# Another listed order for every step of a linear-attention and top-2 expert kernel

## The chip, the cores and the metric

The kernel runs on one core of a Trainium2 chip. The metric is the device time of one execution, in microseconds; less is better. Each version is run several times and compared by its median.

## The reference

The reference has two halves. First comes linear attention with a learned feature map, for 8 batches of 8 heads, 576 positions and 64 channels. Then a layer of four attention experts, of which the gate keeps two for each position:

```python
def phi(x):                       # 64 channels -> 256 features
    proj = einsum('bhsd,df->bhsf', x, w_phi)
    proj = proj - max(abs(proj), axis=-1)
    return concatenate([exp(proj), exp(-proj)], axis=-1)
kv  = einsum('bhsf,bhsd->bhfd', phi(k), v);  z = phi(k).sum(axis=2)
x   = einsum('bhsf,bhfd->bhsd', phi(q), kv) / (einsum('bhsf,bhf->bhs', phi(q), z) + 1e-6)
x   = x.transpose(0, 2, 1, 3).reshape(8, 576, 512)

w   = softmax over the 2 largest of x @ w_gate        # 4 experts
for e in range(4):
    a   = softmax(causal(0.125 * (x @ wq[e]) @ (x @ wk[e]).T))
    out += w[..., e] * (a @ (x @ wv[e]) @ wo[e])
```

All arrays are float32, and the output is 8 x 576 x 512.

## The kernel before, in words

The heads go in 32 pairs, four pairs to a batch. For a pair, TensorE projects the keys (`stream_k`, matmuls of `half_mm` at L501), VectorE centers them (`center`), ScalarE takes the exponentials (`phi_k`), and TensorE multiplies them with the values (`stream_kv`, L642). The last 64 keys of each head go two pairs at a time through `stream_tails` (also L501) and `tail_products` (L607). The sum over keys is needed too. For the first four pairs (batch 0) TensorE makes it from all keys. From pair 4 on `key_sum` makes most of it elsewhere: gpsimd starts a transfer that adds one half of the keys' features into `zs` (a transfer `zs<-ek`), VectorE adds two parts of `zs` (L582), gpsimd adds the tails (a transfer `zs<-ekt`), and TensorE only sums the result over partitions (L654). For the queries, TensorE projects (`stream_q`, L501), ScalarE or VectorE copies the result out (`evac_u`), gpsimd reduces over partitions, and two exponentials follow (`phi_q`). TensorE then makes denominators and numerators (`stream_n`, L740 and L751), and `divide` writes a pair's part of x.

When four pairs are done, `stream_b` projects the batch's x to q and k (`proj_t`) for two experts at a time, makes their scores (`scores`, L871), and projects v and the gate (`proj_v`). These projections and the last one to the output run through the helper `mm` (L294). Two experts' scores make a group, so there are 16 groups, 0 to 15. A group's causal scores lie in four sets of two PSUM banks, one bank an expert (`BANKS`): the first set has 512 columns, the second 256, the third 320, and the last 512, of which the last 64 count in 64 rows only. `evac_s` copies each bank to `s`; `mask` (gpsimd) fills the upper triangle; `maxima` takes a running maximum over key blocks (VectorE, L992), reduces it over partitions (gpsimd, L996) and subtracts it (VectorE, L1000); `expo` takes the exponentials in place (ScalarE, L305); `add_up` (VectorE, L1012) and `sums` (TensorE, L1038) make the divisor; `attend` multiplies with v (TensorE, L1067), `evac_y` scales and splits the result, and `project_out`, `evac_o` and `store` bring it out.

All of PSUM is one pool of eight banks of 512 float32 (`ps_c`). A step that needs a bank gets the one that was released longest ago, by the plan's own reckoning; TensorE waits if the copy that empties it is not done. Until the first x is complete, `keep_warm` multiplies a tile of ones in bursts of three matmuls.

The order of the work is written down. Each piece of work is a generator, and each `yield` in it is a step on one engine. `ORDER` is a string with one character a step, the place of the generator in the list of live ones. `SIDES` has one character for each copy that may go to ScalarE (0) or VectorE (1). `Plan.loop` (L225) replays both; a change to one character would change the meaning of all behind it, since a generator that ends leaves the list. `in_order` (L245) then pins each engine's instructions in the order in which they were made:

```python
for c in ORDER:
    s = self.streams[ord(c) - 48]
    st = s[1]
    if isinstance(st.eng, tuple):
        st.eng = st.eng[int(next(sides))]
```

Transfers are issued by SP, the first two loads of q by ScalarE, and the adding transfers by gpsimd. Each engine works through its own list and waits by semaphores for the data that it needs from the others.

Of the kernel before, what the change touches and what calls it, by code (L numbers as in the profile page):

```python
# [68 lines left out]


ORDER = (
    r'111111110432049269C8GD4FF79FCB53DDD2D987CEG0FIE8=D4H9B1FDBBHFF9DIHFEF=C=8I7JIFH99EFI5CL0CL8B2DBBB=D=E=EED>4B36'
    r'7=BIK=ICE8=HIIHDGEG>DGGEF5:>:2>9=I:KJCHBE=7:F=DBD:9:JF25DGFH=F=:FED>8H2>>E446:HHHJHHADB<7HHG8:5<AG:3H9JFMBBFBJ'
    r'A9GFCE0FA;<<88@:CE;7JACCIG<LI:CC;7@GI993::6KDJKHH:IDHD?BA:DGG??:;?9;GEEGF0DD;AGEEADD40CC@B?B01<96877;;;DA?=C4;'
    r'GHH8D=G=6==852;8:@30C>8IAD?CCCC?BC998CB;;6D>BF?CAF@GGCBE8A9F408F58A77FJ8IDJ?F;88KFFJ;3;BPLLH?JKB=HH18;GC;;:I;H'
    r'BIHHHCCCH6;JJ;2828BHH>6G@BGF8;5;>D=EECC=::8DHGHCGCC::<G>GFDE@H999JCJC?C03888808IC8HKJI:@68P8BHBFCIK<LBED7H5FIJ'
    r'JE83IF7IJF?K>FF:999=8JJLG?LE>C=88>A8=7EIJ?28AGA7BEGHII=FI8GG139>9>?6H9EHD8J8F75B4I87L<G20G?CK@DDFGGD<8<FE86H=G'
    r'8?D998:86?DHHIJG::IJJ<HI:7K7I:L:?M<C<IDC?F>????H:B>JKMK<;;MJ;8BJILL<FD:G:=8HIFLLI:JH::J58E86H0I8813KKIFA:L@IHN'
    r'H:>EIEII<EGEL<IDFGDEE=DE=DH;;<D:H:<ICKKIH@KGH>HFF<E6<<GDD@DDDDFDEEEE<K:CK:DIMLLG:20488N98ND?DL8EHLKI::5LMCC==L'
    r'FDPB<TI3AFQRBGL8LLFG9?990BBGD>FHHHDDLB8@E>;@@8@HB@AHJBB@AEC8@?CI=ABC>AEB982;;@7<7@DH88FE8=E>>>GFGD<DC83997=D8?'  # L80
    r'?88JI5GGH2B76?LFA8KHIH8F8H8LF9BE98GGJKKK8K;GIII1DEH=F5778083CH488=EHM2<D6JHKE6FA<I?IDH8CH::::::J98EHHKHD6:HL?G'
    r'HIJCHHDGFEGG99CH?BH88EFE7E?8GGE:8G88:GE?:J@7IGLI?G5BF:CKNPMMF@J=22=83180AFAA9;B;:::JCJECGB=D:E:JFL>K0FEECEKDCD'
    r'6GLJ<FIGEI?FE<<<<:DC<?NHHHFDGDCHCDED88:I=HGD::IFJBC>E8<<HB:JEDJEIF6D5LE9989G8K88347O7BCFKJH8EKCGCD;@KIG<M??MJH'
    r'C8GG688OCAKBGDG0J8=KA9998AID@32DH@DA57GING>GIJJJ>AE>JGLKFGG@>>>E848>E80I899F7DK>IBDFJDCC7E@=F=8;;=D==G9DCNED88'
    r'88L<FB57J6OL?I6MMJ3GJH<<:CGH:::0818282:OC:NEBDC=NMNDCCCJFI99:IFCHCFHH:FF7FA7;I8LH8CJICFE8IK::LE8:LML>5LFGCEE=:'
    r'6:EDB==NIKIKLNKEL<GC::GGJCBCGI:FC;;98=8=FG1D=DD=83C88F8DEBBFEFBH8I56E<8J=BKJJE=B6E?EEBB<<<@<B=@@::E99CCDFCC@88'
    r'48LLDK@;9CBMF=2>:G:A80388KH=KMFK=CJI88D83:<JCG?6@E99KCLL?8KCE977KLILL57IJLI8MN88D8HI72IM8LH88N<MKH9L@BGFCCL@GG'
    r'J9>920K<LKIDE?B=GG=F7H:<:<>:H=<L?KLAD::LIJF=KEI7L65D=DDDGE99K=DJFII77<DLFM6JJOKEC==CD=:K:<<G<<BG<ABL388488NL1M'
    r'KHFLM0<8CLEN8>8A8J56CNQNQ>GB80;;8F=AI8DE883IGHCJ::KO28KD;:LFD>LDDFGK:::DD=:QI:J6J@DCGFN=DFGIF:>>JDFCKHCEDHD9;;'
    r'688:DDDC=EGGEDCFF@:8IGC<:D5KD::FL<CONAKALALECCCOONKFAAO@<C>B=MAE@DNG@<H<DAAAA?LAA<??99DHAFGI@81B3DM20HF848C889'  # L90
    r'@IJCE?C<GB<HIHF>8A8AB87>DF>8C7;H5IFED6MA@MF<F<<G?99KC8<3F8I89?820JKJ8>4D<KFH88?>GDEGGE77999>L8>LF<CCFCD57DJLAG'
    r'2@3081>88LDEGEE8D<>ECC8FC9;;IDGB7B6ECJ<6@CHB::::K<DDBI::LD<DAKCFGD:BGE>C869KM>LFLL8A8BI8I81@7FA996I7AHB2701>GK'
    r'49HHBGK9J9KAK=FAG69AA<M5AFEDF9997G<<EK<A@DECHBCA1@H@B8@B@:AEGB@@@F;::IH779<=HICCC4EG@@CE=?B;;C=?DD7<EC=@;A;AK?'
    r'CHC;9E5BDCBCCDA99CJ98827770KDH<>GCC>7L8??C>@A?H>>GK3FEK>KLEF0HF=I@66GE<;?6BB>6F@@CCG<6@D=5<5:3<C@9:CH?@?EDC<@7'
    r'E7;;71?AFE66FCF>;055E=@1BB8@744255AD>>D?E4A4CB?B@7>A0444453?@3D:E8;=A?=2BA>=122<6DAA;54=966=482E94:4@@1:735DE5'
    r'331D6CCGBF;;1@8<6>333CBD3<3;3I>D>E=<3@7C9337;<<<<B9?D6=8@?=<A7?2:<;<21;2:71:?:1AA=;;::>1<===44766835510=84<?;4'
    r'>8>8747804=4>2020697=0=87086@A5:<966>1=;811027708?>90269>=<;9C<9<>>0>5<:;5555<<B9:4711=>067?0@7566<=>>>058464<'
    r':<0<;939629922133357642000;5:00<;0873228;::893061166855809590:99900105<58=:5898986558090085807:70:669581661660'
    r'00155665A558=06<1<A@1<<66><768<1673157246485665524223114114314571131733544334289112297742551554100341311231231'
    r'2012100007=<=<=<61310;21189534233403402200'  # L100
)
# [1090 lines left out]
```

## Time and profile before

| | before |
|---|---|
| median of 3 runs | 586.99 us (586.22 to 588.25) |
| the profiled execution, own time | 586.51 us |
| its span on the chip | 584.6 us |
| mean granted TensorE clock | 0.998 |

The profiled execution is one run. Its span is what the profiler's records cover, and its own time is 1.9 us more. It lies 0.48 us under the median of the timed runs. "Busy" on TensorE is time with a matmul in flight. The clock is told as a share of full speed, and stands at full speed nearly throughout.

The rows that the prediction uses follow in a section of their own. In them a line number such as L501 is a line of the kernel, or of a helper through which several parts go; the tile names after it (out<-in, buffer numbers left out) tell which part it is.

### The profile page before, as it was taken

To read this page: it belongs to the slowest core of one execution; us is meant where nothing else is said; L and a number is where in the kernel's file an instruction comes from. 1 tells how busy PE (TensorE), PEld (TensorE's weight loads), DVE (VectorE), ACT (ScalarE), POOL (GpSimd) and SP (SyncE) were. 2 spreads that over 40 slices of the span, in tenths; PEclk is the share of its full clock that TensorE was granted. 3 is DMA by queue.
4 is the path that set the end of the run, shared out by engine and by line. 5 is a ranking of instruction groups with operands and counts; after the bars stand their busy time and mean duration, and the time that the engine had idled before them with its cause. 6 is when DMAs were issued, how large, how long until landed. Compare 5 with 4: busy or idle time off the path is not lost.

```text
span 584.6 us, 19211 instructions
## 1 busy us (share of the span) xinstructions
PE 574.3 (98%) x7667; PEld 442.3 (76%) x7667; DVE 532.2 (91%) x1145; ACT 453.0 (77%) x1114; POOL 291.2 (50%) x223
## 2 busy tenths in 40 slices
PE   8999999999999999999999999999999999999996
PEld 6664787677976789667886777966888678878885
DVE  6999898999999999999899998999898998898994
ACT  4998869868797959878769788688887877776652
POOL 4536473676545572265654375535556546331520
PEclk9999999999999999999999999999999999999999
DMA  5669475643645663564565446367453832311013
GB/s 151 164 159 214 108 159 131 140 106 66 129 133 109 153 176 77 136 152 118 137 143 133 108 131 135 97 141 190 99 124 81 195 97 33 70 40 71 1 43 123
DMA packets 55049, 69.75 MB, mean 119 GB/s; under 512 B 29232, under 2 KB 32688, under 8 KB 54960
## 3 DMA queue, kind: packets, MB, share of 16 engines
q1 hardware_dynamic: 48368, 49.58, 29.7%
q0 software_dynamic: 6272, 18.35, 19.2%
q8 instruction: 61, 1.00, 0.7%
q10 hardware_dynamic: 320, 0.59, 0.4%
q14 instruction: 28, 0.23, 0.1%
HBM read 35.59 MB, written 14.55 MB: 86 GB/s over the span
## 4 chain that ended last, share of the span: by engine, by line
PE 86%; DVE 5%; DMA 4%; ACT 2%; POOL 1%; issue 1%; SPq 1%; ACTq 0%; POOLq 0%; DVEq 0%
PE ps_c L294 32%; PE ps_c L501 12%; PE ps_c L751 10%; PE ps_c L642 9%; PE ps_c L871 7%; PE ps_c L1067 7%; PE ps_c L740 5%; PE ps_c L607 1%; PE ps_c L654 1%; PE ps_c L1038 1%; DMA q_in<-in_qt_dram 1%; DMA zs<-ek 1%; DVE s L1000 1%; DMA zs<-ekt 1%; DVE top L992 1%
## 5 line engine op out<-in xcount | busy, mean ns | idle before, releaser
L713 POOL PARTITION_ALL_REDUCE mx<-u x64 | 142.4, 2248 | 52.3 <-DVE s L1000 17.0
L294 PE MATMUL ps_c<-x,qk 128*128 128x256 f32 (+1 forms) x768 | 107.8, 298 | 0.0
L294 PEld LDWEIGHTS ps_c<-x,qk 128*128 128x128 f32 x768 | 102.6, 189 | 4.6 <-issue 1.7
L979 POOL TENSOR_SCALAR_AFFINE_SELECT s<-s 128x256 f32<-128x256 f32 (+1 forms) x80 | 48.6, 629 | 98.6 <-ACT s L303 44.2
L996 POOL PARTITION_ALL_REDUCE max<-top x16 | 57.4, 3589 | 32.1 <-DVE top L992 16.6
L305 ACT ACTIVATE ek<-ek 128x1024 f32<-128x1024 f32 x64 | 67.9, 1063 | 4.3 <-DVE ek L569 3.8
L1000 DVE TENSOR_TENSOR s<-s,max 128x1152 f32<-128x1152 f32 (+4 forms) x80 | 64.6, 842 | 0.4 <-POOL max L996 0.4
L303 ACT COPY u<-ps_c 128x256 f32<-128x256 f32 (+1 forms) x118 | 45.0, 402 | 22.2 <-PE ps_c L501 22.0
L642 PE MATMUL ps_c<-ek,v_in 128*32 128x256 f32 x1024 | 61.7, 381 | 0.0
L303 ACT COPY s<-ps_c 128x448 f32<-128x448 f32 (+4 forms) x135 | 50.1, 427 | 12.4 <-PE ps_c L871 12.1
L305 ACT ACTIVATE s<-s 128x640 f32<-128x640 f32 (+4 forms) x80 | 57.6, 742 | 2.6 <-DVE s L1000 2.5
L294 PE MATMUL ps_c<-yh,wo 128*128 128x256 f32 (+1 forms) x256 | 52.8, 300 | 0.0
L715 DVE TENSOR_TENSOR u<-u,mx 128x576 f32<-128x576 f32 x64 | 49.9, 789 | 0.8 <-POOL mx L713 0.8
L642 PEld LDWEIGHTS ps_c<-ek,v_in 128*32 128x32 f32 x1024 | 31.2, 110 | 23.7 <-issue 4.8
L294 PE MATMUL ps_c<-vg,x 128*128 128x260 f32 x384 | 49.0, 285 | 0.0
L331 POOL DMA_DIRECT2D zs<-ek x28 | 25.9, 925 | 44.1 <-ACT ek L305 14.5
L294 PEld LDWEIGHTS ps_c<-vg,x 128*128 128x128 f32 x384 | 47.2, 188 | 0.5
L566 DVE TENSOR_REDUCE pmax<-ps_c 128x4 f32<-128x512 f32 x64 | 42.7, 678 | 5.3 <-PE ps_c L501 4.4
L1067 PE MATMUL ps_c<-s,vs 128*32 128x320 f32 (+4 forms) x896 | 46.6, 357 | 0.0
L305 ACT ACTIVATE mx<-u 128x576 f32<-128x576 f32 x64 | 43.3, 686 | 3.2 <-DVE u L715 3.0
L331 POOL DMA_DIRECT2D zs<-ekt x28 | 24.0, 858 | 43.5 <-DVE zs L582 31.4
L501 PE MATMUL ps_c<-q_in,wf 64*128 64x256 f32 (+1 forms) x256 | 42.7, 436 | 1.8 <-DMA q_in<-in_qt_dram 1.7
(133 smaller groups left out, 1361.8 us busy)
## 6 DMA issues: line engine op xcount, KB each, us to landing
zs<-ek POOLq DMA_DIRECT2D x28, 512.0 KB, 5.3
out_dram<-ot SPq DMA_DIRECT2D x32, 288.0 KB, 2.5
q_in<-in_qt_dram SPq DMA_DIRECT2D x60, 144.0 KB, 3.3
k_in<-in_kt_dram SPq DMA_DIRECT2D x64, 128.0 KB, 3.7
v_in<-in_v_dram SPq DMA_DIRECT2D x32, 256.0 KB, 3.3
kvd<-kvt SPq DMA_DIRECT2D x104, 48.0 KB, 2.6
kv<-kvd SPq DMA_DIRECT2D x26, 192.0 KB, 2.9
zs<-ekt POOLq DMA_DIRECT2D x28, 128.0 KB, 3.4
```

The source lines that it names most:

```text
L294: nc.tensor.matmul(o, a, b, start=start, stop=stop, skip_group_check=True)
L303: nc.scalar.copy(o, i)
L305: nc.scalar.activation(o, i, func, **kw)
L331: nc.gpsimd.dma_start(o, i, accum_op=ALU.add)
L501: nc.tensor.matmul(o, a, b, start=True, stop=True, skip_group_check=True)
L642: nc.tensor.matmul(o[g, 0:2], v_in[:, 4 * h + t, k:64:2], ek[:, t, :, h, :].rearrange("p c (w f) -> p c w f", w=4), start=False, stop=t == ...
L713: nc.gpsimd.partition_all_reduce(M, U, 128, bass_isa.ReduceOp.absmax)
L715: dve(S, [uk], [mk], port=True).tensor_tensor(out=U, in0=U, in1=M, op=ALU.subtract)
L751: nc.tensor.matmul(ps[g:g + 32, 0:n], kvi[:, 2 * k + (h ^ p % 2), 32 * c:32 * c + 32], P_[h][c][:, s0:s1], start=c == 0, stop=c == 1, skip ...
L996: nc.gpsimd.partition_all_reduce(big.rearrange("p e s -> p (e s)"), top.rearrange("p e s -> p (e s)"), 128, bass_isa.ReduceOp.max)
L1000: dve(2 * (S - 128 * j), [('d', x, j)], [('max', z)], 1.11, True).tensor_tensor(out=block(s_, j, None, rows(j)), in0=block(s_, j, None, ro ...
L1067: nc.tensor.matmul(ps[r:r + 32, q0 - s0:s1 - s0], vs[:, j, 128 * g + 64 * e + k:128 * g + 64 * e + 64:2], ss[x][:, e, o + q0:o + s1], star ...
```

## The change

Only the two strings are others. The same generators run with the same instructions, tiles, transfers and waits; they come in another order on every engine, and some of the copies that may go to either engine go to the other one. The first line of each string:

```diff
 ORDER = (
-    r'111111110432049269C8GD4FF79FCB53DDD2D987CEG0FIE8=D4H9B1FDBBHFF9DIHFEF=C=8I7JIFH99EFI5CL0CL8B2DBBB=D=E=EED>4B36'
+    r'12111111049938C2BC4FFBDD7926DC4ED8G9GG8BF57D0HHB0=9DD9BCCKFBB=FDC34=EE89B1HGH=CDIH=2B79>HII65DM=2CBBIKF=CCC7JE'
...
 SIDES = (
-    r'00000000001010010001110000000000000000011010000001000010001000010000001001100000001000000000000000010000000000'
+    r'11110000010110000000110000001000000100011000000001001000000010000001000000000000000000000000000000000000000000'
...
```

Here is what this moves at two places.

The first place is TensorE's list around pair 4, the first pair whose key sum is made by gpsimd's transfers. `ekt`, `vt_in` are the tails of pairs 4 and 5 and their values, `kt_in` the next tails (of pairs 6 and 7), `ek0` and `v_in` pair 4's features and values, `zs` its key sum, `k_in0` the keys of pair 6. Before:

```order
L607 MATMUL ps_c5_68<-ekt0_111,vt_in_110 32x2x4x32
L607 MATMUL ps_c1_64<-ekt0_111,vt_in_110 32x2x4x32
L501 MATMUL ps_c6_69<-wf_117,kt_in_109 128x128
L501 MATMUL ps_c3_66<-wf_117,kt_in_109 128x128
L642 MATMUL ps_c5_68<-ek0_107,v_in_106 32x2x4x32 x16
L654 MATMUL ps_c5_68<-zs_114,ones_115 32x4x32 x4
L501 MATMUL ps_c7_70<-wf_117,k_in0_102 128x128
```

With the change:

```order
L607 MATMUL ps_c6_69<-ekt0_111,vt_in_110 32x2x4x32
L607 MATMUL ps_c0_63<-ekt0_111,vt_in_110 32x2x4x32
L501 MATMUL ps_c1_64<-q_in0_104,wf_117 128x320
L501 MATMUL ps_c3_66<-q_in0_104,wf_117 128x320
L642 MATMUL ps_c6_69<-ek0_107,v_in_106 32x2x4x32 x16
L654 MATMUL ps_c6_69<-zs_114,ones_115 32x4x32 x4
L501 MATMUL ps_c4_67<-wf_117,k_in0_102 128x128
...
L501 MATMUL ps_c2_65<-wf_117,k_in0_102 128x128
L501 MATMUL ps_c5_68<-wf_117,kt_in_109 128x128
L501 MATMUL ps_c3_66<-wf_117,kt_in_109 128x128
```

The projection of the next tails (`kt_in`) stood ahead of the products of pair 4 and stands now behind the key sum and the projection of the next keys. In its old place stand two matmuls of a query projection.

The second place is ScalarE's list behind the scores of group 15, the last one. `s0` holds group 14, `s1` group 15, `top0` is group 15's running maximum, `yh1` a part of the attention's result. The rows left out are copies of the last set of banks (448 and 64 columns). Before:

```order
L305 ACTIVATE s0_153<-s0_153 128x2x576
L303 COPY s1_154<-ps_c5_68 128x512
L303 COPY s1_154<-ps_c3_66 128x512
L305 ACTIVATE s0_153<-s0_153 128x2x448
L305 ACTIVATE s0_153<-s0_153 128x2x320
...
L305 ACTIVATE s0_153<-s0_153 128x2x192
L305 ACTIVATE s0_153<-s0_153 64x2x64
L303 COPY top0_155<-s1_154 128x2x128
L303 COPY s1_154<-ps_c1_64 128x256
L303 COPY s1_154<-ps_c6_69 128x256
```

With the change:

```order
L303 COPY s1_154<-ps_c6_69 128x512
L303 COPY s1_154<-ps_c5_68 128x256
L305 ACTIVATE s0_153<-s0_153 128x2x576
L305 ACTIVATE s0_153<-s0_153 128x2x448
L305 ACTIVATE s0_153<-s0_153 128x2x320
...
L305 ACTIVATE s0_153<-s0_153 128x2x192
L303 COPY top0_155<-s1_154 128x2x128
L303 COPY s1_154<-ps_c7_70 128x320
L305 ACTIVATE s0_153<-s0_153 64x2x64
L303 COPY s1_154<-ps_c3_66 128x320
L303 CAST yh1_172<-ps_c0_63 128x320
L303 COPY s1_154<-ps_c1_64 128x256
```

The first exponential of group 14 comes behind two copies of group 15's scores instead of ahead of all of them. Of the first set (512 columns) ScalarE copies one bank, where it copied two. Of the second set (256 columns) one copy has moved to the top; the other stands last, and two copies of the third set (320 columns) and a cast have come ahead of it.

## Rows read from the trace of the kernel before

**Rows 1.** the page, engines' busy time; then shares of the chain that ended last

```profile
PE 574.3 (98%) x7667; PEld 442.3 (76%) x7667; DVE 532.2 (91%) x1145; ACT 453.0 (77%) x1114; POOL 291.2 (50%) x223
...
PE 86%; DVE 5%; DMA 4%; ACT 2%; POOL 1%; issue 1%; SPq 1%; ACTq 0%; POOLq 0%; DVEq 0%
```

**Rows 2.** busy time of the engines in stretches: TensorE, its weight loads, VectorE, ScalarE, gpsimd

```profile
0.00:15.00 15.00, 12.47 (x135) 9.85 (x139) 9.37 (x36) 7.53 (x15) 7.30 (x9) 1.00 0.57 147
...
100.00:150.00 50.00, 50.00 (x714) 35.87 (x707) 48.47 (x108) 38.78 (x105) 30.27 (x23) 1.00 0.54 115
...
250.00:300.00 50.00, 49.42 (x659) 38.22 (x656) 45.24 (x93) 40.90 (x98) 31.44 (x21) 1.00 0.55 127
```

**Rows 3.** what TensorE waited for: us in total, times, longest

```profile
PE ps_c L501 <- DMA q_in<-in_qt_dram: 1.7, 2, 1.1
PE ps_c L654 <- DMA zs<-ekt: 1.2, 1, 1.2
...
PE ps_c L961 <- DVE col L952: 0.5, 1, 0.5
PE ps_c L1038 <- DVE max L1012: 0.5, 1, 0.5
```

**Rows 4.** the chain in order of time (start, us, what): steps with and without a hand-off

```profile
18.31 1.31 PE ps_c L501 x8
...
59.77 1.17 PE ps_c L501 x8
...
444.04 2.51 PE ps_c L871 x36
...
536.12 2.78 PE ps_c L871 x35
```

**Rows 5.** TensorE in order of time, first 20 us (start, us, what)

```profile
1.06 2.74 PE L294 MATMUL ps_c<-warm 128*128 128x128 bf16 x24 [1.06 <-DVE col L338]
4.93 2.29 PE L501 MATMUL ps_c<-q_in,wf 64*128 64x256 f32 x8 [1.13 <-DMA q_in<-in_qt_dram]
...
14.12 1.94 PE L642 MATMUL ps_c<-ek,v_in 128*32 128x256 f32 x32
...
19.55 0.34 PE L294 MATMUL ps_c<-warm 128*128 128x128 bf16 x3
```

**Rows 6.** the first key sum, in the chain; then its last steps on TensorE

```profile
40.15 6.43 DMA zs<-ek
...
47.84 5.02 DMA zs<-ekt
...
49.22 0.73 PE L501 MATMUL ps_c<-wf,kt_in 64*128 64x128 f32 x4
49.88 1.94 PE L642 MATMUL ps_c<-ek,v_in 128*32 128x256 f32 x32
53.00 0.43 PE L654 MATMUL ps_c<-zs,ones 128*32 128x128 f32 x8 [1.18 <-DMA zs<-ekt]
```

**Rows 7.** the page, transfers: KB each, median us to landing

```profile
zs<-ek POOLq DMA_DIRECT2D x28, 512.0 KB, 5.3
...
zs<-ekt POOLq DMA_DIRECT2D x28, 128.0 KB, 3.4
```

**Rows 8.** TensorE, then ScalarE, behind the scores of group 15

```profile
549.97 0.28 PE L871 MATMUL ps_c<-ql,kkh 64*128 64x256 f32 x2
...
548.95 1.17 ACT L305 ACTIVATE s<-s 128x1152 f32<-128x1152 f32 x1 [1.12 <-DVE s L1000]
550.02 1.05 ACT L303 COPY s<-ps_c 128x512 f32<-128x512 f32 x2
...
554.41 0.65 ACT L303 COPY s<-ps_c 128x256 f32<-128x256 f32 x2
```

**Rows 9.** VectorE, then gpsimd, in the same stretch

```profile
555.16 1.20 DVE L992 TENSOR_TENSOR top<-s 128x896 f32<-128x896 f32 x1 [0.26 <-ACT s L303]
...
558.48 3.58 POOL L996 PARTITION_ALL_REDUCE max<-top  x1 [3.06 <-ACT vs L303]
```

More of the change, by code (lines that the diff above doesn't have):

```diff
@@ L71 @@
 ORDER = (
-    r'111111110432049269C8GD4FF79FCB53DDD2D987CEG0FIE8=D4H9B1FDBBHFF9DIHFEF=C=8I7JIFH99EFI5CL0CL8B2DBBB=D=E=EED>4B36'
[L73 to L100, printed above, removed]
+    r'12111111049938C2BC4FFBDD7926DC4ED8G9GG8BF57D0HHB0=9DD9BCCKFBB=FDC34=EE89B1HGH=CDIH=2B79>HII65DM=2CBBIKF=CCC7JE'
@@ new lines @@
+    r'I=B8G4=DH>C:>:E>9D8GFHFEF5FCFG:=F=ICF2G:GFHB=:7G9H::EBIB5EEE3==DBD0==C7=31GIK<C9HHGAG863GFG5GEE@;7BC@8;GHGECA;'
+    r'HFE7@B<<C<JIAHDEDHH8;29941CCEIEFF@8;9;I;G6::794@3K:JEIIE00E>>>>8::?B9GA1AFCDFF9:D2FE>74CCDD@7<<BB?@<><8FHBD85?'
+    r'>B6F;;A:;=>AGFFFD?C8@3DE0A6DF8FE8C@CC998;6=CE>>EHDC?BEFE898E5AB7B>87EDIHI>;BBC;CH600JBHBB;;;;;=DGGG;?38;:>EE?E'
+    r'EDDEFDDFFDG>FED?=BC?C?>84A81828288;5E:KA8AGBAD>::?HB@K6::IEJJHBB:EB?FBDHBG9B99?0D8I3888886H<H78IMBJKKGHJ8IFE?8'
+    r'H6D3<:C57EKLN>99J88OJD><F88JI8K=98B7<J?<B<?AHHJI7A22>?@EF@F9<=I998AADEE<=614BF5GGC<FGF@877K3JF8<KKE=IED=ED99=A'
@@ new lines @@
+    r'<H888800:8H6CHI<JIH::CIHBH:7G7G@HJKLH=:6:D==<<;:GJGKBJM<;8BOGGHHGG?BGH:<8:JJ88J:J::J6LMGNAKLA=5;:::KLQMH=II?F@'
+    r'F::LE382480881F==FEL@F8IF=K=DEJEDDD?GJD;CC>H;EFHF9<E=<FBCEBHC?BBB@BCB<BDACA<<;HECC@H@F@8JCIHFJIA::BAGBF8:5F:JH'
+    r'I=LLAC?JI?E?9<LJB@@3G9K9FE?FCDDD?B@B?A@828H880AG>I?DGD@B<F@@EG>>8BD>D>;9G;<FGF<AG@DE=B@C98887C=@D7@EC978=DBGG<'
+    r'=5AEHIE@GDGCD3792888G89<8A8@JF8A768EEIHIJKJ;EAH@F38884FG::75:CE1EJ=BE=::6<<I>2O28=008:EE9=HG6KIF@?FDDE@JJEA==I'
+    r'DH:8@6BBCF8CD9CB98CEBC:D<D8:BF7EA:DDHGB@>CGGBDH=:5:7A=@GOG>@>9;;QPCIIID:E8F:08=CJCN>DC@:M8884IEBBEBHLBJK:<:<KG'
@@ new lines @@
+    r'I=BBEE6BAID=?CC@@@ED@<CC<3<<C6IAH<DHH8HCED8E:::G8>A:NKJEJDGLK5OPO99;19>EBAC83KDLKGFK7HLC7JI88A88A@@@BIIHDIJLIK'
+    r'8FHF629<CA9KCAMLJ88=9IGDD8HHJAA5E=FGBG6H7M???KM6=1JE@FGGFF>9239@DE?I780F888C7FJ>??>>H?>88;DJ=CFJJEGF;L9ALM?EAC'
+    r'FG8<I:5:8<<028887:@843IHI@G:N:O:>EFGBIOOGNBECL99D>LC8KEKBJII@IA8AA=AA::G78IA8KJB=F8AA8::7HJHK:C4J5?AHLK6:::@DQ'
+    r'R@@PNMMCJHEONBFE@:KC;@:I@CGGC=FHE?B;<9FGEFF888302=08GHAF6=68;8IJC15>3GFCCBDKHK<DIEEH8?<<;<<9E98288D8G8BBBCKFEE'
+    r'EEEE<::LDF:8K>MEC9A8<8KCAA:87GJJBKKL>G:<6IAHKCH999O>ONM4O88H>LML7SRKL583SSLSS8C8K727898UW@=S@<<O89L0823R?9B@C?'
@@ new lines @@
+    r'?A>KBLKKDFF@@DG>@CI>@>@G==7:::::<<=AF6F6H?HEBE<5H@GJAH?9EH?B97?EG881=FGFEGE?H=7HD7FFFLJE:E<D<<=MHME<=?D<>:AH80'
+    r'I8BKIH<<<8IJHH;O8M8G865PN=HA=BKLL0;MJJ18::K8883JCLL6:NKK;:::6OFPPMFAQLIKF>DIJCF@=JHDE:FH>=:HGG:EEGIFJJEI9EF>?G'
+    r'@DFD;E:GG28FC8;088:F:FHFF:GJDCI?BC5<:OBB@<OFKAGGJIDIO=CMG<GD<DDBMML<<@AA9>@9FICCCAERAA9I8888304LFHJDIAGEFCHJAC'
+    r'EE7D8>2@@J@CFFIHHHGAG@88J8D=IGBFE=78CG>59938>@I888=A2G=G9IIJ@HFH8CFFG8776=OGOG9ING;9GJE8MJ?KGD8JC38EA824I88975'
+    r'DIJ<>7<<BPFHEFK6LDNKFCF1AF20D6>CE>>C;:;9:9::CD:::HD<JJF<8AGIBEIIBDEJHG8688DLFGLE:D?DAH=BG8G7:@FK?:GI:KJMLC6I:5'
@@ new lines @@
+    r'::C=FI:C:K@LCLE@J>==A:AL=BGJHCCB?BBA>@A@A;A?AC?>??;9<;;@C8830EBCAA88C048@8=@87??5>EE@=6B@<@<<J?D<FE>>@DKG<?>CC'
+    r'B8=>F:CEEFGC?CHHH::G:B@I301BAKG>I?<888<>O77?D77@<BD0;D?<;H6F>G6?FJH6<LDH??E@6?>6?35@=BF:BAB=FEE:CFEE4A57;H;77@'
+    r'G=D;EAID;6=I<:?BF6::EC:E166?697767F<B0A<DBC5E@A<?A?@<55510=@73=43A=BA@8@836351II964HH21E4=2@BFF13>9A<3FE5<EDC:'
+    r'>B;;5@B7A3113<C3?E=A333D3AF>E???8GEEBCB333>D>@?D:=;91?87;>=@872?;2A=;<1;<>2411;;14A?>@10@@>69053942?7:6?4A::9<'
+    r'==5444AA4@793284688669000=8222::51:9>B91D=74?9<1979A6D7C>;@<;86::8>>4<7;0=0<068555==01000@6@67??@>?@>9650>06>>'
@@ L101 @@
+    r'?5>9389;;6;8362800262400803092337679820:916;18<9;8365570050568701:7:9;9590009786587057750775697566666114466554'
+    r'4444300<00<?50:44>=6=841<844772264745511518766454211124421111163841245230<<32322>2;:1;;::102017143133455434321'
+    r'21000>457>=>=010<1;016124422344400423200'
 )
 SIDES = (
-    r'00000000001010010001110000000000000000011010000001000010001000010000001001100000001000000000000000010000000000'
-    r'00000000000000101000000000000000000000000000000000000000000000100100001110100010110000000000001000100000000000'
@@ L106 @@
-    r'00100000000000000000000000000101011000010000000000010000000100000000000000000001000000010000110000000110000000'
-    r'10010000000000000010000000000000000100000010000000001000000000101100000000000000000000000000000001000001000001'
-    r'00000000000010000000000000000001000000110000001000000010001000000000100001100110'
+    r'11110000010110000000110000001000000100011000000001001000000010000001000000000000000000000000000000000000000000'
+    r'00000000000000010000000000000000000000001000000000000000100000000011000100001000010000000000000000000000000000'
@@ L109 @@
+    r'00001000000001000010000101100000000000000000000000000001010001000000000010000000000001011000000000010000001000'
+    r'00100000000000000000000101000000010010000000000010000000010000000001100000000000000000000000000100100000010101'
+    r'00001010000000000000000000001000000100100000001000000000000000000000010010100110'
 )
```

## The prediction

> **What bounds the kernel now.** I read the shares first. TensorE has a matmul in flight for 574.3 of 584.6 us, and 86% of the chain that ended last is its work [rows 1]. The stretches say the same: 50.00 of 50 us in a middle stretch (49.42 in the worst of eight such), and 2.5 us idle in the first 15 us [rows 2]. Then I read what TensorE waited for. The view names little: 1.7 us for the first q tiles, 1.2 us for a key sum, 0.5 us for the gate's column and 0.5 us for the last sum of exponentials [rows 3]. So the order is already close to back to back on the engine that ends last, and a new order can win only what lies between its steps: those named waits, and short hand-offs of a PSUM bank, which show as a longer step and not as a wait. The projection of q over 8 records takes 1.17 us where its banks are free and 1.31 us where TensorE stood waiting for a bank that the copy of kvt had held; a whole group of scores takes 2.51 us, and 2.78 us where the copies of its own first bank freed the banks of its last [rows 4]. That is 0.14 us a hand-off, or 0.27 us where two fall into one step.
>
> **The base.** Durations come from one profiled execution: span 584.6 us, its own time 586.51 us. The three timed runs have a median of 586.99 us, 0.48 us more. My sum is made against 586.51; a measurement of this kernel tells about 0.3% (1.8 us) from no change.
>
> **The change, part by part.**
>
> *Work.* Every product, exponential, transfer and reduction stays, and TensorE changes the shape of its tiles about as often: 212 changes of kind in its list before, 213 now. Two things are not the same. The keep-warm matmuls fall from 33 to 27, and 65 instead of 69 of the copies that may go to either engine go to VectorE (copies of scores 13, were 23; copies of u 18, were 10). By the two sizes of such a copy on ScalarE (0.53 and 0.33 us [rows 8]), four fewer save VectorE about 1.7 us. It is busy 91% and ends nothing by itself [rows 1]: I take 0. If TensorE's work did not cover it, 1.7 us would be the most it could give, and as much the most that ScalarE could lose.
>
> *Keep-warm matmuls.* The first burst has 24 before, 18 now. It ends at 3.80 us, and the first q tile lands only at 4.93 us [rows 5], so its six fewer matmuls cost and give nothing. The three that stand behind the projections of pair 3 before now stand further up, ahead of the first product with keys and values, where TensorE waits for the exponentials of pair 0 in any case (it starts that product at 14.12 us, when they are done, and the chain up to there has the same links in both lists). So the second stretch is shorter by their 0.34 us [rows 5]: **-0.3 us**.
>
> *The first key sum.* From pair 4 on, gpsimd adds two transfers into zs, VectorE adds between them, and TensorE sums the result. The first transfer runs from 40.15 to 46.58 us (40.15 + 6.43), the second from 47.84 to 52.86 us (47.84 + 5.02), and TensorE starts at 53.00 us after its one wait of 1.2 us [rows 3, 6]. In the new list the projection of the next key tails (0.66 us from 49.22 to the next step at 49.88 [rows 6]) stands behind that sum instead of ahead of it. The chain itself has the same links, in the same order on ScalarE, VectorE and gpsimd, so the sum cannot start sooner by it; 0.66 us of cover is taken away and has to be done afterwards. Bounds: +0.66 us if the transfers land as late as now; -1.2 us if they land as fast as the middle of their kind, 5.3 and 3.4 us against the 6.43 and 5.02 us here [rows 6, 7], which gives back the whole wait. SP's list puts the loads of the last weights behind two other loads now, but they still fall into the same stretch, so I take the end at which the rows stand: **+0.66 us**.
>
> *The last group of scores.* This is where ScalarE's order matters. Behind the scores of group 15 the next link is the running maximum on VectorE; its first instruction reads the second bank (256 columns) of both experts. Before, ScalarE copies that bank at 554.41 us, behind the exponential at 548.95 us and what stands between, and VectorE starts the maximum at 555.16 us after 0.26 us of waiting for it [rows 8, 9]. In the new list the exponential stands behind two copies of scores, the second of which needs matmuls that end at 550.25 us [rows 8], so it starts about 1.7 us later, near 550.7 us. Behind it the two 512-column copies are gone (1.0 us), but two copies of 320 columns and one cast of y stand ahead of the last bank copy instead (about 1.1 us by the pace of the same rows), and one copy of that bank has moved up (0.3 us). So the bank is complete about 1.4 us later, the maximum on VectorE too, and with it gpsimd's reduction that started at 558.48 us [rows 9] and the subtraction behind it. TensorE's own steps from there on are the same set; before, it waited 0.5 us twice [rows 3]. I take **+1.0 us** at the last sum, nearer the upper end because the rows stand there, and below it because the three parts of 1.1 us are priced by the pace of other sizes. Bounds: -1.0 us if ScalarE catches up, since then both waits can go; +1.4 us if nothing is absorbed. Everything behind the last sum (two products, sixteen half output steps, four stores) has the same steps and the same two stores in flight: 0.
>
> *Bank hand-offs in the middle.* I walked both TensorE lists, gave each matmul the mean step that its form has in the trace, and took for each reuse of a PSUM bank the work that lies between the last matmul into it and the first of its next user. Under 1.0 us, where copying out can hardly be done in time, there are 18 such reuses before and 13 now; under 2 us 123 and 116. Five fewer at 0.14 to 0.27 us [rows 4]: **-1.0 us**, bounds 0 and -1.4 us.
>
> *Sum:* -0.3 + 0.7 + 1.0 - 1.0 = +0.4 us; 586.51 + 0.4 = 586.9 us, within 0.1 us of the old median. The bounds together run from -3.9 us to +1.8 us.
>
> **A rule weighed.** The named rows say that TensorE is full: 98% of the span [rows 1]. The Trainium skill, "Perfetto Trace Analysis", section "Identifying the Most-Contended Engine", says that the share of time with a matmul in flight is no good measure of how full TensorE is, and that weight loads and the useful rate should be read instead. Weight loads are busy 76% here [rows 1], so by that rule a quarter of TensorE is open, and a better order could win far more than my sum allows; that is the third rival below. The trace agrees with the rule only in part: steps of the same kind repeat to 0.14 us wherever they stand [rows 4], so their length is set inside the step, not by the order.
>
> **The rivals.**
>
> 1. *Hand-offs give more (582.3 us).* If the new order frees not five but all 18 tight reuses, at 0.2 us each, the middle gives 3.6 us instead of 1.0; and if ScalarE catches up at the end too, the tail is -1.0 us. The time is then 586.51 - 0.3 + 0.7 - 1.0 - 3.6 = 582.3 us (584.3 us with the tail as I take it). For it: 10 score copies fewer on VectorE, the engine with least room, and the minimum distance of projections and scores is longer in the new list. Against it: 13 tight ones are still there.
>
> 2. *Key sums run short (590 us), the slower side.* The place is the wait of TensorE for the key sums of pairs 4, 5 and 9 of the list's 28. The work that TensorE has between those pairs' keys and their sums is 1.4, 1.1 and 1.0 us less than before, by the same walk. Before, the first of them was already late by 1.2 us [rows 3]. If all three chains end no sooner than now and had no room left, 3.5 us are added, the other terms cancel (-0.3 + 1.0 - 1.0), and the time is about 590 us. It decides from the point at which the second transfer takes over 5 us as it did at 47.84 [rows 6]; at the middle value of 3.4 us [rows 7] only the first is late, and my forecast holds.
>
> 3. *TensorE is not the limit (about 575 us).* Then the order would work against VectorE's 532.2 us [rows 1], 52 us below the span; a fifth of that is 10 us. Against it stand the rows of the steps [rows 4] and the 0.5 us that VectorE made TensorE wait at each named place [rows 3].
>
> That the change does not do what it says is small here: the lists differ in nearly every place, and what is not "the same instructions" (keep-warm, engine of the copies) is priced above at 0.3 us.
>
> **How the numbers follow.** Forecast: 0.38, all of it within 0.3% of the old median (585.2 to 588.8 us). Rival 1: 0.34, of which 0.02 reach so little that they count as no change. Rival 2: 0.23, all of it slower. Rival 3: 0.05. So faster is 0.32 + 0.05 = 0.37, same 0.38 + 0.02 = 0.40 less the 0.01 that I give to a tail worse than its bound = 0.39, slower 0.23 + 0.01 = 0.24. The range must hold 8 in 10: it leaves out rival 3 (0.05) and the outer parts of rivals 1 and 2 (about 0.07 each): 581.5 to 591.0 us.
>
> **What would show it.** In the changed profile: TensorE again busy 98%, and the waits named for it again under 6 us in all. The keep-warm burst with 18 matmuls, and the first q step no sooner than 4.9 us. The first key sum's wait longer than 1.2 us, by up to 0.7 us. The first running maximum of group 15 on VectorE behind a wait for ScalarE of about 1.5 us (0.26 us before), and the wait at the last sum nearer to 1.5 us than to 0.5 us. Steps of q and of scores with 1.31 and 2.78 us seen more seldom. The prediction is wrong if a middle stretch of 50 us shows TensorE idle for over 1 us, if the key sums of several pairs appear among the waits, or if TensorE's total busy time itself falls by more than 2 us.

## The result: slower by 0.7%

| | before | with the change |
|---|---|---|
| median of 6 runs | 586.61 us (586.07 to 588.25) | 591.42 us (589.91 to 591.87) |
| ratio, 95% interval | | 1.0072 [1.0053, 1.0092] |
| the profiled execution, own time | 586.51 us | 590.68 us |
| its span on the chip | 584.6 us | 588.7 us |

The change costs 4.8 us by the medians, 4.2 us by the ratio; differences further on are by the ratios. The predicted time was 586.9 us, and the range ended at 591.0 us.

The page of the changed kernel, busy times and shares of the chain (against [rows 1]):

```profile
PE 574.3 (98%) x7661; PEld 442.3 (75%) x7661; DVE 525.4 (89%) x1140; ACT 457.1 (78%) x1119; POOL 284.0 (48%) x223
...
PE 85%; ACT 6%; DVE 5%; DMA 2%; issue 1%; POOL 1%; ACTq 0%; DVEq 0%; POOLq 0%
```

TensorE is busy for 574.3 us, as long as before, to the tenth. The span is 4.1 us longer. So TensorE does not work longer in sum: it stands still longer. (That the two sums agree to the tenth is chance, as the stretches below show.)

To see where, I cut both executions at the same two places of the program: the first projection of x for batch 0, and the first scores of group 14, the last but one. Here are the stretches of before, then those of the change (length, TensorE, its weight loads, VectorE, ScalarE, gpsimd, granted clock, share of the transfer engines, GB/s):

```profile
0.00:60.87 60.87, 56.93 (x857) 36.96 (x857) 52.70 (x123) 50.40 (x105) 32.30 (x24) 1.00 0.69 167
60.87:536.05 475.18, 474.43 (x6293) 367.30 (x6291) 440.95 (x938) 378.56 (x943) 245.69 (x187) 1.00 0.51 120
536.05:579.90 43.85, 42.89 (x527) 38.06 (x520) 38.14 (x84) 23.62 (x66) 13.23 (x12) 1.00 0.11 42
```

```profile
0.00:62.52 62.52, 57.68 (x851) 37.53 (x851) 51.67 (x124) 50.25 (x101) 32.55 (x25) 0.97 0.70 169
62.52:538.16 475.64, 473.66 (x6294) 366.55 (x6292) 436.47 (x935) 381.87 (x949) 239.81 (x187) 1.00 0.51 119
538.16:584.20 46.04, 42.95 (x526) 38.22 (x520) 36.41 (x82) 24.26 (x68) 11.63 (x12) 1.00 0.12 47
```

The start is 1.65 us longer, the middle 0.5 us, the end 2.2 us. Idle time of TensorE is the length less its busy time: 3.9, 0.8 and 1.0 us before (5.7 us in all), 4.8, 2.0 and 3.1 us now (9.9 us). In the middle TensorE is busy for 0.8 us less than before, but idle for 1.2 us more. In the start it is busy for 0.75 us more, though it has six keep-warm matmuls fewer: there the granted clock is 0.97 in the mean (the last section shows where it fell).

What TensorE waited for in the changed kernel (us in total, times, longest), against [rows 3]:

```profile
PE ps_c L1038 <- DVE max L1012: 2.9, 3, 1.2
PE ps_c L654 <- DMA zs<-ekt: 2.1, 1, 2.1
PE ps_c L501 <- DMA q_in<-in_qt_dram: 1.6, 1, 1.6
...
PE ps_c L294 <- DVE widey L762: 1.0, 1, 1.0
PE ps_c L961 <- ACT s L305: 0.8, 1, 0.8
```

The sums of exponentials (L1038) waited once before, for 0.5 us; now three times, for 2.9 us. A wait of 1.0 us for VectorE's transpose (L762) is new. All of these waits end on VectorE, which has less to do than before (525 us, was 532). So I read what VectorE waits for. First before, then the change (us in total, times, longest):

```profile
DVE top L992 <- ACT s L303: 0.3, 1, 0.3
```

```profile
DVE top L992 <- ACT s L303: 6.9, 5, 2.1
...
DVE top L315 <- POOL s L979: 2.9, 1, 2.9
```

This is the finding. Before, the running maximum waited 0.3 us for a copy of scores on ScalarE, once. Now it waits 6.9 us, in five of the 16 groups. Group 3 shows how that reaches TensorE. ScalarE, VectorE and TensorE of the changed kernel, in order of time (start, us, what):

```profile
169.95 1.07 ACT L305 ACTIVATE ek<-ek 128x1024 f32<-128x1024 f32 x1
170.91 1.15 ACT L305 ACTIVATE zs<-ek 128x512 f32<-128x512 f32 x2
172.09 1.06 ACT L305 ACTIVATE ek<-ek 128x1024 f32<-128x1024 f32 x1
173.05 0.35 ACT L303 COPY s<-ps_c 128x256 f32<-128x256 f32 x1
...
173.51 1.09 DVE L992 TENSOR_TENSOR top<-s 128x896 f32<-128x896 f32 x1 [2.09 <-ACT s L303]
174.52 0.47 DVE L762 STREAM_TRANSPOSE widey<-ps_c 128x288 f32<-128x288 f32 x1
...
171.17 0.56 PE L1038 MATMUL ps_c<-max,ones 128*32 128x224 f32 x8
...
175.05 0.51 PE L294 MATMUL ps_c<-yh,wo 128*128 128x256 f32 x2 [1.00 <-DVE widey L762]
```

The copy of the second set (256 columns) stands in ScalarE's list behind the exponentials of a pair of keys, 3.1 us of work. VectorE's maximum waits for it. Behind the maximum in VectorE's list stands the transpose that frees the bank of group 2's sums. Its data is there from 171.7 us (171.17 + 0.56), but it starts at 174.52, and TensorE stands 1.0 us for that bank. The Trainium skill, "PSUM — Partial Sum Buffer", section "Engine vs sequencer instructions", says that the queues of VectorE and ScalarE are strictly first in, first out; these rows agree, with 2.8 us between ready and start. So a copy that feeds only the maximum held up a transpose that has nothing to do with it.

This copy did not change its engine. Before, ScalarE did it too, but had both copies of that set done by 163.78 us (163.41 + 0.37), and the maximum started without a wait. ScalarE, then VectorE, before:

```profile
163.41 0.37 ACT L303 COPY s<-ps_c 128x256 f32<-128x256 f32 x1
...
170.15 1.08 DVE L992 TENSOR_TENSOR top<-s 128x896 f32<-128x896 f32 x1
```

The end of the program, ScalarE, then VectorE, against [rows 8, 9]:

```profile
552.84 2.63 ACT L305 ACTIVATE s<-s 128x1152 f32<-128x1152 f32 x3
555.38 1.15 ACT L303 COPY s<-ps_c 128x448 f32<-128x448 f32 x4
...
557.61 0.41 ACT L303 COPY top<-s 128x256 f32<-128x256 f32 x1 [0.65 <-POOL s L979]
...
559.07 0.37 ACT L303 COPY s<-ps_c 128x256 f32<-128x256 f32 x1
...
559.54 1.09 DVE L992 TENSOR_TENSOR top<-s 128x896 f32<-128x896 f32 x1 [1.56 <-ACT s L303]
560.55 0.28 DVE L1012 TENSOR_TENSOR max<-max,s 64x128 f32<-64x128 f32 x1
```

Counted from the first scores of group 14, the maximum of group 15 starts at 21.38 us (559.54 - 538.16), 2.3 us later than before (555.16 - 536.05 = 19.11). The last addition of group 14 (L1012) stands behind it on VectorE, and TensorE's sums of group 14 need that addition: a gap of 1.1 us that was not there before.

The first key sum, in the chain and then in TensorE's order of time, against [rows 6]:

```profile
46.92 5.81 DMA zs<-ekt
```

```profile
48.85 1.94 PE L642 MATMUL ps_c<-ek,v_in 128*32 128x256 f32 x32
52.87 0.42 PE L654 MATMUL ps_c<-zs,ones 128*32 128x128 f32 x8 [2.08 <-DMA zs<-ekt]
```

The sum starts at 52.87 us, before at 53.00; TensorE is there 1.0 us earlier and waits 0.9 us longer.

### The profile page after: what moved, and what is told of

It is laid out like the page before. It is cut to its first block, busy times and chain, and to the rows that moved or that the text cites. A ratio compares the mean times of both kernels' runs of the same rounds, so it can differ in the third digit from the quotient of the medians.

```text
span 588.7 us, 19227 instructions
## 1 busy us (share of the span) xinstructions
PE 574.3 (98%) x7661; PEld 442.3 (75%) x7661; DVE 525.4 (89%) x1140; ACT 457.1 (78%) x1119; POOL 284.0 (48%) x223
## 4 chain that ended last, share of the span: by engine, by line
PE 85%; ACT 6%; DVE 5%; DMA 2%; issue 1%; POOL 1%; ACTq 0%; DVEq 0%; POOLq 0%
PE ps_c L294 31%; PE ps_c L501 12%; PE ps_c L751 9%; PE ps_c L642 9%; PE ps_c L1067 7%; PE ps_c L871 6%; PE ps_c L740 5%; PE ps_c L654 2%; ACT ek L305 2%; PE ps_c L607 1%; DVE max L1012 1%; DVE top L992 1%; PE ps_c L1038 1%; DMA zs<-ekt 1%; ACT s L303 1%
## 5 line engine op out<-in xcount | busy, mean ns | idle before, releaser
L979 POOL TENSOR_SCALAR_AFFINE_SELECT s<-s 128x256 f32<-128x256 f32 (+1 forms) x80 | 42.4, 578 | 72.2 <-ACT s L303 36.8
L303 ACT COPY s<-ps_c 128x448 f32<-128x448 f32 (+4 forms) x146 | 54.2, 424 | 17.8 <-PE ps_c L871 17.3
L1000 DVE TENSOR_TENSOR s<-s,max 128x1152 f32<-128x1152 f32 (+4 forms) x80 | 63.1, 822 | 0.6 <-POOL max L996 0.6
L294 PE MATMUL ps_c<-yh,wo 128*128 128x320 f32 (+1 forms) x256 | 52.6, 299 | 1.0 <-DVE widey L762 1.0
L303 ACT COPY u<-ps_c 128x256 f32<-128x256 f32 (+1 forms) x110 | 41.2, 401 | 13.9 <-PE ps_c L501 13.7
L715 DVE TENSOR_TENSOR u<-u,mx 128x576 f32<-128x576 f32 x64 | 47.1, 754 | 0.2 <-POOL mx L713 0.2
L501 PE MATMUL ps_c<-q_in,wf 64*128 64x256 f32 (+1 forms) x256 | 44.2, 435 | 1.8 <-DMA q_in<-in_qt_dram 1.6
```

Of the source, the lines that this page charges most:

```text
L294: nc.tensor.matmul(o, a, b, start=start, stop=stop, skip_group_check=True)
L303: nc.scalar.copy(o, i)
L501: nc.tensor.matmul(o, a, b, start=True, stop=True, skip_group_check=True)
L715: dve(S, [uk], [mk], port=True).tensor_tensor(out=U, in0=U, in1=M, op=ALU.subtract)
L1000: dve(2 * (S - 128 * j), [('d', x, j)], [('max', z)], 1.11, True).tensor_tensor(out=block(s_, j, None, rows(j)), in0=block(s_, j, None, ro ...
```

## The experiments

Theory A is what the rows above say: TensorE's added idle time at a few places is the loss, and most of it comes from score copies that stand late in ScalarE's list. Theory B: the loss is spread, by banks handed over later all along. Theory C: it is the key sums, as in the prediction's second rival. Times before stand beside each group of runs, since the same runs of before were shared.

### Which stretch: four orders put together from both

Each takes its steps up to a cut from one kernel's order, and those left from the other's. The cuts are the first projection of x (61 us in the trace) and the projections for the last two experts of batch 7 (about 523 us). At the first the two orders have done the same steps but for six, at the second but for three, and the keep-warm steps.

The late part of the change, and the late part of before:

```diff
-3122 steps in the order of before
+2916 steps in the order of before, the 206 left in that of the change
```

```diff
-3120 steps in the order of the change
+2915 steps in the order of the change, the 205 left in that of before
```

The early part of the change, and its middle:

```diff
-3120 steps in the order of the change
+319 steps in the order of the change, the 2801 left in that of before
```

```diff
-3122 steps in the order of before
+the first 321 and the last 205 in the order of before, the 2596 between in that of the change
```

> The order of before up to the projections for the last two experts of batch 7 (about 523 us), and from there the order of the change. Theory A, idle TensorE: the loss is TensorE standing still between steps, and each stretch loses what its gaps grew by in the two profiles: 1.0 us up to the first scores (about 70 us), 1.2 us in the middle, 2.1 us behind 523 us. So +2.1 us against before (588.7 us), with a gap of about 1.1 us ahead of the sums of group 14 and 1.2 us ahead of those of group 15. Theory B, spread: banks are handed over later all along, so the loss goes with the length of a stretch: +0.5 us here. Theory C, key sums early on: 0 us here.

> The order of the change up to about 523 us, then the order of before. Theory A: +2.2 to +2.7 us against before (about 589.0 us), and the gaps ahead of the last sums back to 0.5 us and less. Theory B: +4.3 us. Theory C: +4.8 us.

> The order of the change up to the first projections of x (about 70 us; keep-warm work, first key sum and weight loads lie in it), then the order of before. Theory A: +1.0 us (587.6 us), nearly all of it in the wait for the first key sum, 2.1 us instead of 1.2 us. Theory B: +0.5 us. Theory C: +4 us or more.

> The order of before up to about 70 us and from 523 us on, that of the change between. Theory A: +1.2 us (587.8 us), as one wait of 1.0 us near 174 us and one of 0.6 us near 457 us come and one of 0.6 us near 273 us goes. Theory B: +3.7 us, and no single gap. Theory C: 0 us.

| | time | ratio to before (586.34 us) |
|---|---|---|
| late part of the change | 589.03 us | 1.0041 [1.0028, 1.0055] |
| late part of before | 587.85 us | 1.0024 [1.0011, 1.0037] |
| early part of the change | 587.49 us | 1.0016 [1.0001, 1.0031] |
| middle of the change | 587.40 us | 1.0011 [0.9998, 1.0024] |

The part behind 523 us costs 2.4 us, the first 61 us 0.9 us, the middle 0.6 us (its interval holds zero). Together 0.68%, where the whole change has 0.72%: the parts add. Theory B wanted 3.7 us from the middle, theory C 4 us from the start; both fall. The first two rows hold complementary parts of the change and make 0.65% together. Theory A had the right places, but not every size: the run with the late part of before costs 1.4 us, where 2.2 to 2.7 us were expected, and the middle 0.6 us instead of 1.2 us.

### One copy, then all of them

From here on each kernel keeps the banks of the order that it starts from (here that of the change), whatever moves: a table SLOTS names them, so that a moved step doesn't deal all later banks anew.

```diff
-                slot = sorted(self.psum[st.tag], key=lambda kt: self.last.get(kt[0], (0.0, ''))[0])[:st.n]
+                slot = [{x[0][1]: x for x in self.psum[st.tag]}[int(next(banks))] for _ in range(st.n)]
```

One copy of group 15, ScalarE's list:

```diff
 L303 COPY s1_154<-ps_c4_67 64x64
+L303 COPY s1_154<-ps_c1_64 128x256
 L305 ACTIVATE s0_153<-s0_153 128x2x192
...
 L303 CAST yh1_172<-ps_c0_63 128x320
-L303 COPY s1_154<-ps_c1_64 128x256
```

> The order of the change with one instruction moved, the banks pinned to those that the change took: ScalarE's last copy of group 15's second set (128 x 256) goes ahead of two copies of 320 columns, a cast and two exponentials. Theory A, a late score copy holds VectorE: the running maximum of group 15 starts at about 558.1 us instead of 559.5, the gap ahead of the sums of group 14 (1.12 us) goes, and the time falls by 1.3 us against the change (590.1 us, +3.5 us against before). Rival, the copies are not what holds it: VectorE's own list in front of the maximum is as late, the time stays at 591.4 us.

Measured: 588.64 us, ratio 1.0046 [1.0030, 1.0063] (before 586.43 us). From 1.0072 that is 1.5 us less for one instruction moved by six places. The two intervals overlap, so the time of this run alone would not settle it; its profile does say more. The gap ahead of group 14's sums is gone, and those behind it stayed.

All such copies, ScalarE's list for group 3 (in groups 12 and 14 the copy moves up in the same way, in group 14 past a cast and the `top` copy); for group 11 a copy on VectorE is recorded two masks earlier, which leaves every engine's list as it was and only makes its wait shorter:

```diff
+L303 COPY s1_154<-ps_c1_64 128x256
 L305 ACTIVATE ek1_108<-ek1_108 128x4x256
 L305 ACTIVATE zs_114<-ek1_108 128x2x256 x2
 L305 ACTIVATE ek1_108<-ek1_108 128x4x256
-L303 COPY s1_154<-ps_c1_64 128x256
```

> As the run before, and in groups 3, 12 and 14 too the last copy of the second set is moved up on ScalarE; for group 11 VectorE's copy of the first block is recorded ahead of two masks that it need not wait for (its place in VectorE's list is the same). Theory A: VectorE's wait for the score copies falls from 6.9 us to under 2 us; TensorE's gaps of 1.0 us near 174, 0.6 us near 457 and 1.1 us near 560 us go; 2.5 to 3.0 us less than the change (588.4 to 588.9 us). Rival: the gaps near 174 and 457 us have other causes, and only the 1.3 us of the run before are gained.

Measured: 586.35 us, ratio 0.9998 [0.9987, 1.0009]. Five edits give back 4.3 us (the two intervals leave about 1.3 us either way), more than the 2.5 to 3.0 us expected, and the kernel is level with before. That does not make it the same as before: its start and its end still lose, and its middle gains, as the last two runs show. VectorE's waits of the maximum in this kernel:

```profile
DVE top L992 <- POOL s L979: 1.6, 5, 0.4
DVE top L992 <- DVE top L992: 0.5, 1, 0.5
DVE top L992 <- ACT s L303: 0.2, 1, 0.2
```

6.9 us of waiting for ScalarE became 0.2 us. TensorE's gaps near 174, 457 and 560 us are gone.

### The key sum: weights loaded later

SP's list; the cast and the subtraction of these weights move back with them:

```diff
-L327 DMA max0_156<-in_wts_dram 64x1024 x2
 L327 DMA v_in_106<-in_v_dram 128x512
 L327 DMA q_in1_105<-in_qt_dram 64x576 x2
 L327 DMA k_in1_103<-in_kt_dram 64x512 x2
 L327 DMA kt_in_109<-in_kt_dram 64x2x64 x2
 L327 DMA q_in0_104<-in_qt_dram 64x576 x2
 L327 DMA vt_in_110<-in_v_dram 64x64 x4
+L327 DMA max0_156<-in_wts_dram 64x1024 x2
```

> The order of the change, banks pinned, with the two loads of the last weights (512 KB) moved on SP from 46 us, ahead of the second transfer of the first key sum, to behind the second key sum, and their cast and subtraction moved back by some 15 us. Theory A for the key sum, shared transfer engines: zs<-ekt lands in 3.5 to 4.5 us instead of 5.9, the gap of 2.1 us falls to about 0.5 us, 1.5 us less than the change (589.9 us). Rival: the other loads of that stretch fill the engines as well, the landing stays over 5 us and the time at 591.4 us.

> Both edits of the two runs before in one kernel. If the gaps add, 4.0 to 4.5 us less than the change: 587.0 to 587.4 us, about level with before (586.6). If a gap only moves to another place, under 3 us less.

Measured: 590.59 us, ratio 1.0075 [1.0052, 1.0098], and with the copies too 586.98 us, 1.0013 [0.9998, 1.0028]. Nothing is gained by the late weights: the copies alone had 0.9998. What TensorE waited for, weights late and copies as in the change:

```profile
PE ps_c L1038 <- DVE max L1012: 2.9, 3, 1.2
PE ps_c L642 <- DMA v_in<-in_v_dram: 1.6, 1, 1.6
...
PE ps_c L654 <- DMA zs<-ekt: 0.6, 1, 0.6
```

The wait for the first key sum did go (the 0.6 us are a pair's near 207 us). TensorE starts it without waiting, 1.8 us sooner than in the change (52.87 us):

```profile
51.05 0.40 PE L654 MATMUL ps_c<-zs,ones 128*32 128x128 f32 x8
```

But the values of the next pair have one buffer, `v_in`; their load starts when the products of pair 4 are through, and TensorE, now early, waits 1.6 us for it instead. The transfer's part of the theory was right, and the gain it promised was not there: the next wait stood 5 us behind.

### The same copies on VectorE

Four characters of SIDES; VectorE's list for group 15:

```diff
 L1081 TENSOR_TENSOR ps_c0_63<-ps_c0_63,rb0_157 128x320
+L315 COPY s1_154<-ps_c1_64 128x256
 L1012 TENSOR_TENSOR max0_156<-max0_156,s0_153 128x2x192
 L992 TENSOR_TENSOR top0_155<-s1_154 128x2x448
```

> The order of the change, banks pinned; the last copies of the second set of groups 3, 12, 14 and 15 stay where they are recorded, but VectorE does them instead of ScalarE (four characters of SIDES). Theory A: the running maximum no longer waits for ScalarE; VectorE pays four copies of about 0.42 us. The waits of the running maximum for ScalarE fall under 1 us, and 3.5 to 4.3 us of the 4.8 us are gained (587.1 to 587.9 us). Rival, it is VectorE that has no room: its list in front of the same sums gets longer, and under 2 us are gained.

Measured: 587.75 us, ratio 1.0024 [1.0011, 1.0037] (before 586.24 us): 2.8 us of 4.2 us gained by the ratios, between the theory (3.5 us and more) and its rival (under 2 us). The time itself lies inside the theory's 587.1 to 587.9 us, but the runs of before that were taken with it were faster than those of the result. VectorE's wait for ScalarE at the maximum is 0.2 us. Group 11 was left alone here, and its wait of 2.9 us for the masks stayed, as did TensorE's gap near 457 us (0.6 us).

### The other way round, and the best of both

In before, one copy of group 15 made late, ScalarE's list:

```diff
 L303 COPY s1_154<-ps_c1_64 128x256
-L303 COPY s1_154<-ps_c6_69 128x256
 L303 COPY vs_166<-ps_c3_66 128x260
 L303 COPY vs_166<-ps_c0_63 128x260
+L303 COPY s1_154<-ps_c6_69 128x256
```

> The order of before, banks pinned, with one instruction moved the other way: ScalarE's last copy of group 15's second set behind two copies of v instead of ahead of them, the first of which waits for TensorE. The copy ends about 3.2 us later, at 558.3 us. Theory A: the running maximum starts 3.0 us later, the gaps ahead of the last sums grow, 2.5 to 3.2 us more than before (589.1 to 589.8 us). Rival, the end of the program has room in it: under 1 us more.

Measured: 589.55 us, ratio 1.0056 [1.0038, 1.0074], 3.3 us more. The maximum started 2.6 us later (557.72 us):

```profile
557.72 1.09 DVE L992 TENSOR_TENSOR top<-s 128x896 f32<-128x896 f32 x1 [3.52 <-ACT s L303]
```

Since the middle of the change keeps TensorE busy for less time, two kernels take it with the copies of groups 3, 11 and 12 mended: one between the start and the end of before, one behind the change's own start and ahead of the end of before.

```diff
-the first 321 and the last 205 in the order of before, the 2596 between in that of the change
+the same, copies of groups 3, 11 and 12 moved up as above
```

```diff
-2915 steps in the order of the change, the 205 left in that of before
+the same, copies of groups 3, 11 and 12 moved up as above
```

> The order of before up to about 70 us and from 523 us on, between them that of the change with the copies of groups 3, 11 and 12 moved up; banks pinned to those of the run with the middle of the change. Theory A: the gaps of 1.0 us near 173 and 0.6 us near 457 us go, and the middle of the change is then better than that of before: 585.2 to 585.9 us, 0.5 to 1.2 us less than before. Rival, the gaps only move: 587.0 us or more.

> The order of the change with the copies of groups 3, 11 and 12 moved up until 523 us, then the order of before; banks pinned. Against the run with all copies moved up, the two last gaps (0.93 and 1.20 us) should go back to 0.5 us each. Theory A: 585.0 to 585.6 us, about 1 us less than before. Rival, the start of the change (its longer wait for the first key sum) costs what the end gains: 586.4 us.

Measured: 584.06 us, ratio 0.9964 [0.9949, 0.9980], and 584.64 us, 0.9978 [0.9963, 0.9992]. The first is 2.1 us faster than before and the fastest kernel of this study; 0.5 to 1.2 us were expected. It differs from the run with the middle of the change (1.0011) only by the copies of groups 3, 11 and 12: they are worth 2.8 us. The two new runs differ from each other only by the start, and the second from the run with all copies moved up (0.9998) only by the end. So the change's start costs 0.8 us, and its end, with its copies mended, still 1.2 us; these two differences are no larger than the intervals. What TensorE still waits for in it:

```profile
PE ps_c L654 <- DMA zs<-ekt: 1.4, 2, 1.0
PE ps_c L501 <- DMA q_in<-in_qt_dram: 1.1, 1, 1.1
...
PE ps_c L501 <- DMA k_in<-in_kt_dram: 0.8, 1, 0.8
PE ps_c L961 <- DVE col L952: 0.5, 1, 0.5
PE ps_c L1038 <- DVE max L1012: 0.5, 1, 0.5
```

## Why the prediction was wrong

*The frame held.* TensorE is the engine that ends last, its work is the same in both orders, and an order wins or loses only what lies between the steps. In sum all 4.1 us of the span are that. But the equal busy sums hide two opposite changes, 0.75 us more in the start and 0.77 us less in the middle.

*Work, and with it ScalarE's order outside the last group: this is the step that failed.* The prediction counted how many copies each engine has (of the score copies 23 on VectorE before, 13 now) and took 0 for it, since VectorE "ends nothing by itself". Where a copy stands in ScalarE's list was priced only behind group 15. No count shows this loss: the four late copies, of groups 3, 12, 14 and 15, are on ScalarE in both kernels and only stand later in its list. The question was what stands ahead of them there, and who waits behind the waiting maximum on VectorE. In five groups the maximum stood for 0.2 to 2.1 us, and other work stood behind it. The run with the copies moved up shows the size of it: 4.3 us, 1.0072 against 0.9998. Of these, 2.8 us lie in the middle (groups 3, 11 and 12), for which the sum had nothing: it forecast 1.0 us less there, and 0.6 us more were measured. One of the five edits is not a late copy but a copy that waited for masks (group 11, TensorE's gap of 0.6 us near 457 us); this one had moved from ScalarE to VectorE.

*The last group of scores: right place, wrong size.* Predicted +1.0 us with a bound of +1.4; the end took 2.2 us more in the profile, 2.4 us by the run with the late part alone. The exponential did start 1.8 us later, as priced (1.7). But the time from there to the end of the last copy was to shrink by 0.3 us and grew by 0.5 us (6.11 us before, from 548.95 to 555.06; 6.60 us now, from 552.84 to 559.44): ScalarE's `top` copy waits 0.65 us for gpsimd's masks, a wait that the sum left out. The one copy of group 15 that then came last is worth 1.5 us. And the sums of group 14, one group ahead, were taken to be safe; their last addition stands behind the late maximum on VectorE.

*The key sum: right mechanism, a little small.* Predicted +0.66 us with the sum starting no sooner; the wait grew by 0.9 us, and the sum starts within 0.13 us of where it did. The early part alone measured 0.9 us.

*Bank hand-offs: the gain came, larger than its bound, and its mechanism is only half seen.* Predicted -1.0 us in the middle, with -1.4 us as the most. TensorE is busy there for 0.8 us less, which was hidden under 1.2 us of new waits; with those mended the kernel is 2.1 us faster than before. The shorter time is in the steps, as forecast: the scores (L871) keep TensorE busy for 41.93 us of the middle, 42.76 before. The one step of q of 1.31 us is gone from the chain. But long steps of scores are not rarer: there 2.67, 2.77 and 2.78 us stand beside one of 2.53, where two of 2.78 stood beside one of 2.51. That the five reuses counted are the cause is not shown. *Keep-warm:* the first burst gave nothing, as said; of the 0.3 us of the second stretch at most 0.13 us can be left, since the first key sum starts only that much sooner.

*The signs that it named.* The maximum of group 15 stands behind a wait of 1.56 us for ScalarE (about 1.5 us forecast), and the last sums behind one of 1.2 us: that part of the mechanism is as it said. But TensorE's named waits are 9.7 us in all, not under 6 us. And from 150 to 200 us TensorE is idle for 1.0 us, just the bound that it gave for being wrong; the wait of group 3 lies there.

*The rivals.* The second gave 590 us and came near by luck, in another way: it wanted waits at the key sums of pairs 4, 5 and 9, and the profile has one, of 2.1 us. The third (575 us, TensorE not the limit) fell: TensorE's matmul share stayed at 98% while the time moved by 4.8 us, and the best order that was tried is at 584 us. Whether the rule that it leaned on holds is neither shown nor refuted by that.

## What to carry to other kernels

When an order changes, don't price it by the sums of busy time or by counts of copies: look for the engine that waits for each moved step, and list what stands behind that wait. A short copy that feeds a long chain belongs ahead of long work that nobody waits for yet. One look at "what VectorE waits for, by line" shows it (0.3 against 6.9 us); in the shares of the chain VectorE stayed at 5%, and ScalarE went from 2% to 6%. Removing a wait pays only up to the next one; name that one first.
